# Another order table and other PSUM turns for the opening of an attention and feed-forward kernel

## The chip, the cores and the metric

The kernel runs on one core of a Trainium2 chip. The metric is the device time of one execution in microseconds (us); the time before is the median of three runs.

## What is computed

Causal attention in blocks of 64 positions over 8 batches, 8 heads, 576 positions and 64 features, and then a feed-forward layer on the 4608 tokens (512 to 2048 to 512 features, SiLU between):

```python
scores = scale * np.matmul(q, k.transpose(0, 1, 3, 2))
mask = block_i >= block_j
scores = np.where(mask, scores, -1000000000.0)
scores = scores - np.max(scores, axis=-1, keepdims=True)
attn = np.exp(scores)
attn = attn / (np.sum(attn, axis=-1, keepdims=True) + 1e-09)
return np.matmul(attn, v).astype(np.float32)
...
h = x @ w_in
g = h * (1.0 / (1.0 + np.exp(-h)))
return (g @ w_out).astype(np.float32)
```

The weights come as 64-bit numbers. A weight is a pair of 32-bit words in the kernel's view; it is put together as a 32-bit number on the chip (`rebias` on ScalarE, `bits` on VectorE) and split into a high and a low part (`hi` on ScalarE, `lo` on GpSimd), and each product is the sum of three matmuls of parts.

## The kernel before, in words

Every step of the program has a name, such as `b.norm:1` or `u1.load`, and the string `ORDER` lists all of them, some thousands, in one row. The loop at the end of `attn_ffn` (from L1242) takes them one by one and records their instructions. Each engine, and the SyncE queue (SP) that issues all DMAs, executes its own instructions in that order and waits at the first one whose inputs or buffers are not ready. So the table sets the order on each engine and in the DMA queue, and nothing else is reordered.

The part of the program that this case is about goes as follows.

- `a` and `b` (class `First`, L869) are the attention of the first 64 positions, four batches each. TensorE computes scores (L906), VectorE the maxima (L847, L914) and the differences (L919), ScalarE the exponentials (L924), VectorE sums and reciprocals (L928 to L932), GpSimd multiplies by the reciprocals (`norm`, L935, two per group), TensorE transposes (`turn`, L857; one `turn` reads what both `norm` wrote), ScalarE copies back (L860), TensorE multiplies by v (L947), ScalarE and VectorE make the high and low parts of the tokens (L952, L956).
- `c0` to `c3` (class `Second`, L958) do the same for positions 64 to 191. `BANKS` (L964) says which of the PSUM banks S0 to S3, or U, each of the four groups uses for its two score tiles and for its product.
- `w0` to `w15` are the 16 tiles of the first weight matrix, 512 KB each; `o0` and on are those of the second; `t0` transforms the second matrix's first rows.
- `warm:n` (L827) are matmuls on zeros, n times 64 columns, whose result nobody reads. They fill stretches in which TensorE has nothing to do.
- `ffn` is half of a tile of the first feed-forward product (`ffn1`, L1060). I call them F0, F1, ... in their order; two of them make one tile z0, z1, ... (z12 is F24 and F25, z13 is F26 and F27). `keep` (L1066, ScalarE) copies a finished tile out of one of two PSUM banks, and `save` (L1071, SP) writes it to memory, so `save` waits for `keep` and `keep` for both `ffn`.
- `u0`, `u1`, ... are the heads of the positions from 128 on; `u0.load` and `u1.load` (L668) each fetch 256 KB into one half of the same tile. `d0.run:0` (L766, its matmuls at L775) computes the scores of u0 and u1 together: its first two matmuls of 448 columns read what `u0.load` fetched, the next two what `u1.load` fetched. TensorE therefore waits for both loads before it gets past this step.

A DMA's completion semaphore is one of eight in turn, and the ninth DMA waits for the first to land.

Of the kernel before, what the change touches and what calls it, by code (L numbers as in the profile page):

```python
# [79 lines left out]
w3.bits:2 b.norm:1 warm:17 b.turn:0 w6.load b.turn:1 w0.hi c3.load b.back:0 w2.bits:0 w1.lo c0.scores w2.bits:2 b.back:1 b.pv  # L80
c0.max:0 w7.load w8.load w3.hi w2.hi w4.rebias w9.load w4.bits:0 w0.lo b.hi:0 w5.rebias w10.load ffn c0.exp:0 b.lo:0 w4.bits:2
w4.hi b.hi:1 ffn c0.max:1 w5.bits:0 w5.bits:2 w3.lo c1.load c0.load_v w2.lo ffn ffn c3.scores b.lo:1 keep save w5.hi keep
w7.rebias c0.exp:1 w4.lo w5.lo c3.max:1 c3.max:0 w7.bits:0 w7.bits:2 w6.rebias c0.sum ffn ffn c3.sub:0 ffn ffn keep w6.bits:0
w11.load w8.rebias w6.bits:2 c0.norm w8.bits:0 c0.turn:0 save w9.rebias c3.exp:0 w6.hi c0.turn:1 w8.bits:2 w9.bits:0 w12.load
c3.sub:1 c0.back:0 c0.back:1 c1.scores w7.hi w10.rebias c0.pv keep o0.load w9.bits:2 w6.lo c3.exp:1 w10.bits:0 ffn c3.sum:0
w9.hi w8.hi w10.bits:2 w7.lo ffn w11.rebias w9.lo ffn c3.sum:1 keep w8.lo c3.norm ffn c0.hi w14.load c1.max:0 save c1.sub:0
c1.exp:0 w11.bits:0 w11.bits:2 w14.rebias w11.hi w14.bits:0 keep w11.lo ffn w12.rebias ffn w10.hi w13.load c1.max:1 w10.lo
c1.sub:1 c1.load_v save w14.bits:2 ffn w15.load ffn c1.exp:1 c1.sum:0 c1.sum:1 keep ffn w12.bits:0 w13.rebias w12.bits:2 c1.norm
w13.bits:0 w13.bits:2 ffn save c1.turn:0 o1.load c2.load c1.turn:1 c0.lo c3.turn:1 o0.rebias c3.turn:0 w15.rebias w15.bits:0
o1.rebias w12.hi w12.lo keep c1.back:0 c1.back:1 w15.bits:2 c2.scores o0.bits:0 save w14.hi w14.lo c2.max:0 w13.hi c1.pv w15.hi  # L90
ffn c3.load_v save keep o0.bits:2 ffn ffn c2.exp:0 c2.max:1 save c2.load_v c2.exp:1 save o1.bits:0 w15.lo o1.bits:2 keep w13.lo
all.staged t0.hi:0 t0.hi:1 c1.hi c2.sum c1.lo ffn c3.back:0 c2.norm ffn c3.back:1 keep c2.turn:1 c2.back:1 t0.lo:0 c2.turn:0
c2.back:0 t0.lo:1 t0.x:0 c3.pv c2.pv c3.hi ffn save ffn t0.hi:2 c2.hi save keep u0.load ffn ffn t0.lo:2 t0.x:1 c3.lo keep
o2.load o3.load u0.load_v u1.load_v ffn t0.x:2 t0.hi:3 u2.load_v u1.load u3.load_v save c2.lo save u2.load d0.run:0 keep u3.load
save ffn u4.load u0.max:0 u5.load u0.max:1 u0.ones ffn u0.max:2 u1.max:0 u0.gather ffn u1.ones u0.top keep u1.max:1 ffn
u0.spread u1.max:2 save u0.wide u1.gather ffn u0.sub:0 keep u1.top u0.exp:0 save ffn u0.sub:1 u1.spread u0.sub:2 u0.exp:1
u1.wide ffn u0.add:0 keep u1.sub:2 u0.exp:2 save u1.sub:0 u1.exp:2 u0.add:1 ffn u1.sub:1 u1.exp:0 u0.add:2 u1.exp:1 u0.add:3
d1.run:0 keep u1.add:0 save u1.add:1 ffn u1.add:2 u6.load u2.max:0 u7.load u1.add:3 u2.max:1 u2.ones ffn u2.max:2 u0.sums
u2.gather u3.max:0 ffn keep u2.top u3.ones u3.max:1 save u2.spread u3.max:2 ffn u2.wide u3.gather ffn u2.sub:0 keep u3.top
u2.exp:0 save u2.sub:1 u3.spread u1.sums ffn u2.exp:1 u2.sub:2 d0.sums_g u2.add:0 u3.wide ffn keep u3.sub:2 d0.sums_m u2.exp:2  # L100
save u3.sub:0 u3.exp:2 ffn u3.sub:1 u3.exp:0 u2.add:1 d0.inverse u3.exp:1 d2.run:0 u2.add:2 keep u2.add:3 save u3.add:0 d2.run:1
d0.half u4.max:0 u3.add:1 u4.max:1 u4.ones u3.add:2 u4.max:2 u3.add:3 u4.gather ffn u4.load_v d0.fold u5.load_v u8.load u9.load
u2.sums d0.mult u5.max:0 ffn u4.top u5.ones u5.max:1 u4.spread u5.max:2 ffn keep u4.wide u5.gather save ffn u4.sub:0 d0.x_hi
u5.top u4.exp:0 d0.x_lo u4.sub:1 u5.spread u3.sums ffn keep u4.sub:2 d1.sums_g save u5.wide ffn u4.exp:1 d1.sums_m u5.sub:2
u4.exp:2 u5.sub:0 u5.exp:2 d3.run:0 u5.sub:1 keep u4.add:0 d1.inverse u5.exp:0 save u5.exp:1 u4.add:1 u4.add:2 d3.run:1 d1.half
u6.max:0 u4.add:3 u6.max:1 u6.ones u5.add:0 u6.max:2 u6.gather ffn u5.add:1 u6.load_v d1.fold u7.load_v u10.load u11.load
u4.sums d1.mult u7.max:0 ffn u6.top u5.add:2 u7.ones u7.max:1 u6.spread u5.add:3 u7.max:2 ffn keep u6.wide u7.gather save ffn
u6.sub:0 d1.x_hi u7.top u6.exp:0 d1.x_lo u6.sub:1 u7.spread u5.sums ffn keep u6.sub:2 d2.sums_g save u7.wide ffn u6.exp:1
d2.sums_m u7.sub:2 u6.exp:2 u7.sub:0 u7.exp:2 d4.run:0 u7.sub:1 keep u6.add:0 d2.inverse u7.exp:0 save u7.exp:1 u6.add:1
u6.add:2 d4.run:1 d2.half u8.max:0 u6.add:3 u8.max:1 u8.ones u7.add:0 u8.max:2 u8.gather ffn u7.add:1 u8.load_v d2.fold  # L110
u9.load_v u12.load u13.load u6.sums d2.mult u9.max:0 ffn u8.top u7.add:2 u9.ones u9.max:1 u8.spread u7.add:3 u9.max:2 ffn keep
u8.wide u9.gather save ffn u8.sub:0 d2.x_hi u9.top u8.exp:0 d2.x_lo u8.sub:1 u9.spread u7.sums ffn keep u8.sub:2 d3.sums_g save
u9.wide ffn u8.exp:1 d3.sums_m u9.sub:2 u8.exp:2 u9.sub:0 u9.exp:2 d5.run:0 u9.sub:1 keep u8.add:0 d3.inverse u9.exp:0 save
u9.exp:1 u8.add:1 u8.add:2 d5.run:1 d3.half u10.max:0 u8.add:3 u10.max:1 u10.ones u9.add:0 u10.max:2 u10.gather ffn u9.add:1
u10.load_v d3.fold u11.load_v u14.load u15.load u8.sums d3.mult u11.max:0 ffn u10.top u9.add:2 u11.ones u11.max:1 u10.spread
u9.add:3 u11.max:2 ffn keep u10.wide u11.gather save ffn u10.sub:0 d3.x_hi u11.top u10.exp:0 d3.x_lo u10.sub:1 u11.spread
u9.sums u10.exp:1 u10.sub:2 ffn d4.sums_g u10.add:0 u11.wide u10.exp:2 u11.sub:2 ffn keep d4.sums_m u11.sub:0 u11.exp:2 save
u11.sub:1 d6.run:0 keep u10.add:1 d4.inverse u11.exp:0 save u11.exp:1 u10.add:2 u10.add:3 d6.run:1 d4.half u12.max:0 u11.add:0
u12.max:1 u12.ones u12.max:2 u11.add:1 u11.add:2 u12.gather ffn u12.load_v d4.fold u13.load_v u11.add:3 u16.load u17.load
u10.sums ffn u13.max:0 d4.mult u12.top u13.ones u13.max:1 ffn u12.spread u13.max:2 keep u12.wide d4.x_hi ffn save u13.gather  # L120
d4.x_lo u12.sub:0 ffn u13.top keep u12.sub:1 u13.spread save u11.sums ffn u12.exp:0 u12.sub:2 d5.sums_g u13.wide ffn d5.sums_m
keep u13.sub:2 u12.exp:1 save u13.sub:0 u12.exp:2 ffn u13.sub:1 u12.add:0 u13.exp:0 d5.inverse u13.exp:1 d7.run:0 keep u12.add:1
u13.exp:2 save u12.add:2 u12.add:3 d7.run:1 u13.add:0 d5.half u14.max:0 u14.max:1 u14.ones u13.add:1 u14.max:2 u13.add:2
u14.gather ffn u13.add:3 u14.load_v d5.fold u15.load_v u18.load u19.load u12.sums d5.mult ffn u15.max:0 u14.top u15.ones
u15.max:1 ffn u14.spread u15.max:2 keep u14.wide d5.x_hi ffn save u15.gather d5.x_lo u14.sub:0 ffn u15.top keep u14.sub:1
u15.spread save u13.sums ffn u14.exp:0 u14.sub:2 d6.sums_g u15.wide ffn d6.sums_m keep u15.sub:2 u14.exp:1 save u15.sub:0
u14.exp:2 ffn u15.sub:1 u14.add:0 u15.exp:0 d6.inverse u15.exp:1 d8.run:0 keep u14.add:1 u15.exp:2 save u14.add:2 u14.add:3
d8.run:1 u15.add:0 d6.half u16.max:0 u16.max:1 u16.ones u15.add:1 u16.max:2 u15.add:2 u16.gather ffn u15.add:3 u16.load_v
d6.fold u17.load_v u20.load u21.load u14.sums d6.mult ffn u17.max:0 u16.top u17.ones u17.max:1 t0.lo:3 ffn u16.spread u17.max:2
# [1164 lines left out]
```

## Time and profile before

| | us |
|---|---|
| runs | 939.77, 937.24, 937.60 |
| median | 937.6 |
| profiled execution, device time | 938.08 |
| its span, first to last instruction | 936.4 |
| TensorE busy in the span | 929.8 |

The profiled execution is 0.5 us above the median. 1.7 us of its time lie outside its span. Differences that are worked out inside the span are added to the median. Start times in the trace count from the first instruction. An engine shown as busy may hold a waiting matmul's neighbours only; the weight loads of TensorE (called PEld) show waits more plainly than its matmuls.

### The profile page before, as it was taken

The page shows a single profiled execution, that of the slowest core. Times are in us where ns is not written, and L with a number is a line of the kernel's source. Part 1 is how long each engine was busy: PE and PEld are TensorE (multiplying, and loading weights), DVE is VectorE, ACT ScalarE, POOL GpSimd, SP SyncE. Part 2 cuts the span into 40 slices and gives each one's busy share as a digit, 9 for nine tenths or more (in the row PEclk, how much of TensorE's full clock was granted, in tenths as well). Part 3 has the DMA queues.
Part 4 walks back from the last instruction along what each step waited for, and adds up shares of the span by engine and source line. Part 5 has one row for each costly group of instructions (what it writes and reads, how often), then busy time and mean ns, then how long its engine had stood idle before and what let it go on. Part 6 is the DMA issues. An engine that isn't in the chain of part 4 may idle for free.

```text
span 936.4 us, 23557 instructions
## 1 busy us (share of the span) xinstructions
PE 929.8 (99%) x8646; PEld 815.2 (87%) x8646; DVE 717.8 (77%) x1489; ACT 641.1 (68%) x1621; POOL 550.1 (59%) x799
## 2 busy tenths in 40 slices
...
DMA packets 109813, 139.97 MB, mean 149 GB/s; under 512 B 22656, under 2 KB 87168, under 8 KB 109696
## 3 DMA queue, kind: packets, MB, share of 16 engines
...
## 4 chain that ended last, share of the span: by engine, by line
PE 98%; DVE 1%; ACT 0%; POOL 0%; issue 0%; ACTq 0%; POOLq 0%
PE h L1060 42%; PE c L1143 21%; PE S L1143 16%; PE u L775 7%; PE S L775 5%; PE SC L775 3%; PE U L775 1%; PE h L827 1%; PE S L857 0%; PE S L990 0%; PE U L1029 0%; PE S L1029 0%; PE S L947 0%; DVE p L919 0%; DVE m L914 0%
## 5 line engine op out<-in xcount | busy, mean ns | idle before, releaser
L1060 PE MATMUL h<-x,wi 128*128 128x448 f32 (+2 forms) x1968 | 406.8, 365 | 0.2 <-issue 0.2
L1060 PEld LDWEIGHTS h<-x,wi 128*128 128x128 f32 x1968 | 359.3, 188 | 35.5 <-issue 0.5
L1125 POOL TENSOR_TENSOR wi<-raw,wi 128x512 fp32r<-128x512 f32 (+1 forms) x114 | 115.8, 1031 | 147.8 <-ACT wi L1121 110.5
L1066 ACT COPY g<-h 128x448 f32<-128x448 f32 (+1 forms) x160 | 86.9, 543 | 40.7 <-PE h L1060 27.0
L721 ACT ACTIVATE p<-p 128x448 f32<-128x448 f32 (+2 forms) x192 | 100.9, 571 | 2.2
L775 PE MATMUL S<-qk 64*64 64x384 f32 (+1 forms) x512 | 99.6, 516 | 0.0
L728 POOL TENSOR_TENSOR pa<-p 128x448 f32<-128x448 f32 x64 | 73.3, 1145 | 27.1 <-ACT p L721 15.8
L1143 PE MATMUL c<-ta,wi 128*128 128x256 f32 x684 | 87.0, 276 | 0.0
L1088 ACT ACTIVATE raw<-raw 128x1024 f32<-128x1024 f32 x72 | 76.6, 1065 | 13.5 <-DMA raw<-gdb 10.2
L731 POOL TENSOR_TENSOR pa<-pa,p 128x256 f32<-128x256 f32 (+1 forms) x128 | 79.4, 620 | 10.0 <-ACT p L721 0.4
L1143 PEld LDWEIGHTS c<-ta,wi 128*128 128x128 f32 x684 | 81.8, 188 | 0.0
L1143 PE MATMUL c<-tb,wi 128*128 128x256 f32 x498 | 81.4, 276 | 0.0
L775 PE MATMUL U<-p,v 64*64 64x64 f32 (+4 forms) x768 | 79.8, 354 | 0.0
L775 PE MATMUL u<-p,v 64*64 64x64 f32 (+4 forms) x768 | 78.5, 350 | 0.0
L714 DVE TENSOR_TENSOR p<-S,MR 128x448 f32<-128x448 f32 (+1 forms) x128 | 71.7, 581 | 1.1
L1143 PEld LDWEIGHTS c<-tb,wi 128*128 128x128 f32 x498 | 71.0, 188 | 0.0
L1143 PE MATMUL S<-ta,wi 128*128 128x256 f32 x534 | 70.1, 276 | 0.0
L775 PEld LDWEIGHTS u<-p,v 64*64 64x64 f32 x768 | 43.9, 134 | 29.2 <-issue 24.6
L636 DVE TRANSPOSE_TENSOR_REDUCE Mx<-S 128x14 f32<-128x448 f32 (+1 forms) x128 | 69.3, 576 | 0.0
L1143 PEld LDWEIGHTS S<-ta,wi 128*128 128x128 f32 x534 | 65.0, 188 | 0.0
L1143 PE MATMUL S<-tb,wi 128*128 128x256 f32 x384 | 63.9, 276 | 0.0
L692 ACT COPY Mx<-Mx 64x4 f32<-64x4 f32 x128 | 24.7, 193 | 55.5 <-DVE Mx L636 53.9
...
## 6 DMA issues: line engine op xcount, KB each, us to landing
gdb<-g SPq DMA_DIRECT2D x128, 224.0 KB, 2.3
qk<-in_qk_dram SPq DMA_DIRECT2D x64, 256.0 KB, 4.0
raw<-gdb SPq DMA_DIRECT2D x64, 256.0 KB, 3.3
...
gd<-g SPq DMA_DIRECT2D x32, 256.0 KB, 2.8
...
raw<-gd SPq DMA_DIRECT2D x32, 256.0 KB, 3.4
```

Source lines behind the costliest of these rows:

```text
L636: nc.vector.tensor_reduce(out=out, in_=in_, axis=AX.X, op=op, apply_transpose=True)
L692: nc.scalar.copy(two(Mx[HALF[r], 4, 4 * r : 4 * r + 2], 8), Mx[HALF[r], 3, NQB:].rearrange("p (s r) -> p s r", s=2))
L714: nc.vector.tensor_tensor(out=u.p[:, c : c + w], in0=s[:, :w], in1=u.mb[:, q : q + w], op=ALU.subtract)
L721: nc.scalar.activation(u.p[:, c : c + w], u.p[:, c : c + w], AF.Exp, scale=SCALE)
L728: nc.gpsimd.tensor_tensor(out=u.pa, in0=p[:, :NQ], in1=p[:, ZERO:COLS], op=ALU.add)
L731: nc.gpsimd.tensor_tensor(out=u.pa[:, q : q + w], in0=u.pa[:, q : q + w], in1=p[:, c : c + w], op=ALU.add)
L775: nc.tensor.matmul(o, w, x, start=start, stop=stop)
L1060: nc.tensor.matmul(o, w, x, start=half == 0 and i == 0 or f is None and i == 0, stop=(half == 1 or f is None) and i == len(runs) - 1)
L1066: nc.scalar.copy(g, hs.pop(z)[:, :n])
L1088: nc.scalar.activation(u.raw, u.raw, AF.Silu)
L1125: e.tensor_tensor(out=u.goal(1, k), in0=u.source(k), in1=u.goal(0, k), op=ALU.subtract)
L1143: nc.tensor.matmul(o[:, :HD], *runs[k], start=first, stop=u.q == 3 and n == 5, skip_group_check=True)
```

## The change

The table `ORDER` is replaced from its first step to about the start of the heads `u`; from `d0.run:0` on, the steps stand in the same order as before. The steps are the same ones, with two exceptions: the matmuls on zeros are cut differently (16, 22, 6, 15 and 17 before, now 16, 21, 19, 11 and 9, which is 76 units of 64 columns in both), and the banks of `c0` to `c3` are turned.

```diff
-a.load warm:16 a.scores:0 a.max:0 a.sub:0 a.max:1 a.sub:1 a.scores:1 a.max:2 a.sub:2 a.exp:0 a.max:3 a.sub:3 a.exp:1 b.load
...
+a.load b.load warm:16 a.scores:0 a.max:0 a.max:1 a.sub:0 a.sub:1 a.scores:1 a.max:2 a.sub:2 a.max:3 a.sub:3 a.exp:0 a.exp:1
...
-        BANKS = ((0, 1, 1), (2, "U", "U"), (2, 1, 0), (0, 3, "U"))
+        BANKS = ((1, 0, "U"), (3, 2, 2), (0, 1, 3), ("U", 3, "U"))
```

Three places show what moves. The lines of the changed kernel are lower by one. On ScalarE, from the exponentials of `a` to the copies of `b`, before (p is the tile of `a` or `b`, wm a weight tile being put together, x the tokens):

```order
L924 ACTIVATE p<-p 128x8x64 x2
L531 ACTIVATE wm<-wst 128x512 x2
L860 COPY p<-U_269 128x512
L924 ACTIVATE p<-p 128x8x64 x2
L860 COPY p<-S_268 128x512
L531 ACTIVATE wm<-wst 128x512
L952 CAST x<-S_268 128x2x4x64
```

The same place now:

```order
L923 ACTIVATE p<-p 128x8x64 x2
L530 ACTIVATE wm<-wst 128x512
L923 ACTIVATE p<-p 128x8x64
L530 ACTIVATE wm<-wst 128x512
L923 ACTIVATE p<-p 128x8x64
L859 COPY p<-U_271 128x512
L859 COPY p<-S_270 128x512
```

The two exponentials of `b` now stand ahead of both copies of `a`, and one weight tile's step stands before each of them. On VectorE, in the row of small steps there, before (m is a maximum, rr the sums and reciprocals, SC the scratch bank of the weights):

```order
L914 TENSOR_REDUCE m<-S_268 128x4
L919 TENSOR_TENSOR p<-S_268,m 128x4x64
L914 TENSOR_REDUCE m<-U_269 128x4
L919 TENSOR_TENSOR p<-U_269,m 128x4x64
...
L544 TENSOR_SCALAR SC<-wm 128x512
L928 TENSOR_REDUCE rr<-p 128x8 x2
L931 TENSOR_SCALAR rr<-rr 128x16
```

The same place now:

```order
L913 TENSOR_REDUCE m<-S_270 128x4
L913 TENSOR_REDUCE m<-U_271 128x4
L918 TENSOR_TENSOR p<-S_270,m 128x4x64
L918 TENSOR_TENSOR p<-U_271,m 128x4x64
...
L927 TENSOR_REDUCE rr<-p 128x8
L543 TENSOR_SCALAR SC<-wm 128x512
L927 TENSOR_REDUCE rr<-p 128x8
```

The first two maxima stand together, and a weight tile's step stands between the two sums of `b`. On GpSimd the two `norm` of `a` change places: `a.norm:1`, which needs the second sum, now comes first.

The third place is the SP queue before `d0.run:0`. Before, from the load of u0 (qk is the tile of u0 and u1, v their values, wst in this place the tiles `o2` and `o3`, gd_1_6 and gd_1_7 the memory of z10 to z13):

```order
L1071 DMA gd_1_6_96<-g 128x512
L668 DMA qk<-in_qk_dram 64x1024
L522 DMA wst<-in_moe_w_out_dram 128x512 x2
L674 DMA v<-in_v_dram 128x320
L675 DMA v<-in_v_dram 64x64
...
L668 DMA qk<-in_qk_dram 64x1024
L674 DMA v<-in_v_dram 128x320
L675 DMA v<-in_v_dram 64x64
L1071 DMA gd_1_6_96<-g 128x512
L1071 DMA gd_1_7_98<-g 128x512
```

The same place now:

```order
L667 DMA qk<-in_qk_dram 64x1024
L673 DMA v<-in_v_dram 128x320
L674 DMA v<-in_v_dram 64x64
...
L1070 DMA gd_1_6_96<-g 128x512 x2
L1070 DMA gd_1_7_98<-g 128x512
L521 DMA wst<-in_moe_w_out_dram 128x512
L673 DMA v<-in_v_dram 128x320
L674 DMA v<-in_v_dram 64x64
L667 DMA qk<-in_qk_dram 64x1024
```

The second qk row is `u1.load`. Before, it stood ahead of the saves of z11 and z12; now it stands behind the saves of z10, z11 and z12, behind `o3.load` and behind two DMAs of `u2.load_v`.

## Rows read from the trace of the kernel before

**Rows 1.** Page, part 1: busy time of each engine.

```profile
PE 929.8 (99%) x8646; PEld 815.2 (87%) x8646; DVE 717.8 (77%) x1489; ACT 641.1 (68%) x1621; POOL 550.1 (59%) x799
```

**Rows 2.** Windows, matmuls on zeros (L827): stretch, length, PE, PEld, clock, DMA, GB/s.

```profile
1.05:4.66 3.61, 3.61 (x4) 0.75 (x4) 1.00 0.77 275
16.79:18.76 1.97, 1.97 (x6) 0.73 (x6) 1.00 1.05 386
```

**Rows 3.** Timeline of TensorE, opening: start, length, operation, [idle before, releaser].

```profile
12.78 0.66 PE L857 MATMUL U<-ident,p 128*128 128x128 f32 x4 [1.65 <-POOL p L935]
...
18.76 1.09 PE L857 MATMUL S<-ident,p 128*128 128x128 f32 x8
...
21.75 2.97 PE L1060 MATMUL h<-x,wi 128*128 128x256 f32 x23
```

**Rows 4.** Timeline of VectorE, the sums of a, the differences and sums of b.

```profile
9.67 0.17 DVE L931 TENSOR_SCALAR rr<-rr 128x8 f32<-128x8 f32 x1
...
10.66 0.64 DVE L931 TENSOR_SCALAR rr<-rr 128x8 f32<-128x8 f32 x1
...
12.61 1.28 DVE L919 TENSOR_TENSOR p<-S,m 128x512 f32<-128x512 f32 x2
...
16.20 0.25 DVE L932 RECIPROCAL rr<-rr 128x16 f32<-128x16 f32 x1
```

**Rows 5.** Timeline of GpSimd, the norms of a and b.

```profile
10.23 1.04 POOL L935 TENSOR_TENSOR p<-p,rr 128x512 f32<-128x512 f32 x1 [8.74 <-DVE rr L932]
11.68 1.04 POOL L935 TENSOR_TENSOR p<-p,rr 128x512 f32<-128x512 f32 x1 [0.41 <-DVE rr L932]
16.60 2.05 POOL L935 TENSOR_TENSOR p<-p,rr 128x512 f32<-128x512 f32 x2 [3.88 <-DVE rr L932]
```

**Rows 6.** Timeline of ScalarE, the exponentials of b between weights and copies.

```profile
11.59 0.66 ACT L531 ACTIVATE wm<-wst 128x512 f32<-128x512 f32 x1 [0.64 <-DMA wst<-in_moe_w_in_dram]
...
14.02 1.15 ACT L924 ACTIVATE p<-p 128x512 f32<-128x512 f32 x2
15.07 0.57 ACT L860 COPY p<-S 128x512 f32<-128x512 f32 x1
```

**Rows 7.** Timeline of the SP queue before the heads.

```profile
62.09 0.32 SPq L1071 DMA_DIRECT2D gd<-g  x1
...
63.15 1.00 SPq L522 DMA_DIRECT2D wst<-in_moe_w_out_dram  x2
65.25 0.33 SPq L674 DMA_DIRECT2D v<-in_v_dram  x1
65.62 0.49 SPq L675 DMA_DIRECT2D v<-in_v_dram  x1
...
69.49 0.60 SPq L668 DMA_DIRECT2D qk<-in_qk_dram  x1
```

**Rows 8.** DMA issues of windows from 62.0, 62.4, 69.4 and 72.3: KB, us to landing.

```profile
gd<-g SPq DMA_DIRECT2D x1, 256.0 KB, 2.0
...
qk<-in_qk_dram SPq DMA_DIRECT2D x1, 256.0 KB, 3.6
...
qk<-in_qk_dram SPq DMA_DIRECT2D x1, 256.0 KB, 3.9
...
qk<-in_qk_dram SPq DMA_DIRECT2D x2, 256.0 KB, 4.8
```

**Rows 9.** Timeline of TensorE's weight loads at the start of d0.run:0.

```profile
72.67 0.20 PEld L775 LDWEIGHTS S<-qk 64*64 64x64 f32 x4 [0.36 <-issue]
73.45 0.21 PEld L775 LDWEIGHTS S<-qk 64*64 64x64 f32 x8 [0.58 <-DMA qk<-in_qk_dram]
```

**Rows 10.** Windows of TensorE: d0.run:0 and d1.run:0.

```profile
72.68:75.87 3.19, 3.19 (x49) 1.00 0.92 284
87.01:89.45 2.44, 2.44 (x50) 1.00 0.30 111
```

**Rows 11.** Timeline of ScalarE: the copy that keeps z12.

```profile
70.08 0.59 ACT L1066 COPY g<-h 128x512 f32<-128x512 f32 x1 [2.20 <-PE h L1060]
```

More of the change, by code (lines that the diff above doesn't have):

```diff
@@ L80 @@
[L80 to L129, printed above, removed]
@@ L130 @@
-keep u16.wide d6.x_hi ffn save u17.gather d6.x_lo u16.sub:0 ffn u17.top keep u16.sub:1 u17.spread save u15.sums ffn u16.exp:0
-u16.sub:2 d7.sums_g u17.wide ffn d7.sums_m keep u17.sub:2 u16.exp:1 save u17.sub:0 u16.exp:2 ffn u17.sub:1 u16.add:0 u17.exp:0
-d7.inverse u17.exp:1 d9.run:0 keep u16.add:1 u17.exp:2 save u16.add:2 o2.rebias u16.add:3 o2.bits:0 d9.run:1 u17.add:0 d7.half
-u18.max:0 u18.max:1 u18.ones u17.add:1 u18.max:2 u17.add:2 ffn u18.gather u17.add:3 u18.load_v d7.fold u19.load_v u22.load
@@ L183 @@
[L183 to L185 removed]
+a.load b.load warm:16 a.scores:0 a.max:0 a.max:1 a.sub:0 a.sub:1 a.scores:1 a.max:2 a.sub:2 a.max:3 a.sub:3 a.exp:0 a.exp:1
+a.sum:0 w3.load warm:21 b.scores a.sum:1 b.max:0 w0.load w1.load b.max:1 a.norm:1 a.load_v w0.rebias b.sub:0 b.exp:0 b.sub:1
@@ new lines @@
+w3.lo w4.hi b.lo:1 w2.lo ffn c0.max:1 w5.bits:0 c3.scores keep w5.bits:2 ffn ffn w4.lo w6.rebias w7.load c3.max:1 w5.hi c0.exp:1
+keep w6.bits:0 ffn w6.bits:2 w5.lo c1.load w12.load c3.max:0 c0.sum w6.hi save ffn w8.rebias ffn w8.bits:0 w11.load c3.sub:0
+c0.norm keep w7.rebias w8.bits:2 c3.sub:1 ffn w7.bits:0 c0.turn:0 w10.load w7.bits:2 o0.load w6.lo save c0.turn:1 save c1.scores
+w8.hi w9.rebias w14.load c0.back:0 c0.back:1 c0.pv w9.bits:0 c1.max:0 w7.hi w15.load c1.max:1 keep c1.sub:0 c1.sub:1 c1.exp:0
@@ new lines @@
+c1.exp:1 c3.exp:0 w11.rebias w9.bits:2 w8.lo ffn c1.sum:0 c1.sum:1 w7.lo w11.bits:0 w13.load w11.bits:2 w9.hi ffn ffn w10.rebias
+keep ffn ffn save w10.bits:0 c3.exp:1 c0.hi keep w9.lo ffn w10.bits:2 w10.hi w11.hi c0.lo c2.load ffn c1.norm w10.lo ffn
+c1.load_v w12.rebias w14.rebias save c1.turn:1 c3.sum:0 keep c1.turn:0 c3.sum:1 c2.scores w15.rebias o0.rebias w12.bits:0
+w13.rebias w12.bits:2 c3.norm save w14.bits:0 w14.bits:2 w14.hi c1.back:0 c3.turn:0 c3.turn:1 w13.bits:0 w13.bits:2 c1.back:1
@@ new lines @@
+c1.pv w12.hi w14.lo w15.bits:0 w13.hi keep ffn w11.lo o1.load w15.bits:2 ffn w15.hi c2.max:0 c2.max:1 w15.lo o1.rebias c2.load_v
+o0.bits:0 o0.bits:2 w13.lo ffn c2.exp:0 o1.bits:0 c2.exp:1 w12.lo ffn keep c3.load_v o1.bits:2 c1.hi c3.back:0 all.staged
+t0.hi:0 ffn c2.sum t0.hi:1 save c2.norm t0.lo:0 c3.back:1 o2.load ffn c2.turn:1 keep c1.lo c2.turn:0 save t0.lo:1 save c2.back:1
+c3.pv c2.back:0 keep save c2.pv c3.hi t0.x:0 ffn ffn ffn t0.hi:2 c3.lo ffn c2.hi u0.load keep t0.lo:2 ffn u0.load_v u1.load_v
@@ new lines @@
+t0.x:1 keep save save save o3.load t0.x:2 t0.hi:3 u2.load_v ffn c2.lo u1.load u3.load_v u2.load d0.run:0 keep u3.load save ffn
+u4.load u0.max:0 u5.load u0.max:1 u0.ones ffn u0.max:2 u1.max:0 u0.gather ffn u1.ones u0.top keep u1.max:1 ffn u0.spread
+u1.max:2 save u0.wide u1.gather ffn u0.sub:0 keep u1.top u0.exp:0 save ffn u0.sub:1 u1.spread u0.sub:2 u0.exp:1 u1.wide ffn
+u0.add:0 keep u1.sub:2 u0.exp:2 save u1.sub:0 u1.exp:2 u0.add:1 ffn u1.sub:1 u1.exp:0 u0.add:2 u1.exp:1 u0.add:3 d1.run:0 keep
@@ new lines @@
+u1.add:0 save u1.add:1 ffn u1.add:2 u6.load u2.max:0 u7.load u1.add:3 u2.max:1 u2.ones ffn u2.max:2 u0.sums u2.gather u3.max:0
+ffn keep u2.top u3.ones u3.max:1 save u2.spread u3.max:2 ffn u2.wide u3.gather ffn u2.sub:0 keep u3.top u2.exp:0 save u2.sub:1
+u3.spread u1.sums ffn u2.exp:1 u2.sub:2 d0.sums_g u2.add:0 u3.wide ffn keep u3.sub:2 d0.sums_m u2.exp:2 save u3.sub:0 u3.exp:2
+ffn u3.sub:1 u3.exp:0 u2.add:1 d0.inverse u3.exp:1 d2.run:0 u2.add:2 keep u2.add:3 save u3.add:0 d2.run:1 d0.half u4.max:0
@@ new lines @@
+u3.add:1 u4.max:1 u4.ones u3.add:2 u4.max:2 u3.add:3 u4.gather ffn u4.load_v d0.fold u5.load_v u8.load u9.load u2.sums d0.mult
+u5.max:0 ffn u4.top u5.ones u5.max:1 u4.spread u5.max:2 ffn keep u4.wide u5.gather save ffn u4.sub:0 d0.x_hi u5.top u4.exp:0
+d0.x_lo u4.sub:1 u5.spread u3.sums ffn keep u4.sub:2 d1.sums_g save u5.wide ffn u4.exp:1 d1.sums_m u5.sub:2 u4.exp:2 u5.sub:0
+u5.exp:2 d3.run:0 u5.sub:1 keep u4.add:0 d1.inverse u5.exp:0 save u5.exp:1 u4.add:1 u4.add:2 d3.run:1 d1.half u6.max:0 u4.add:3
@@ new lines @@
+u6.max:1 u6.ones u5.add:0 u6.max:2 u6.gather ffn u5.add:1 u6.load_v d1.fold u7.load_v u10.load u11.load u4.sums d1.mult u7.max:0
+ffn u6.top u5.add:2 u7.ones u7.max:1 u6.spread u5.add:3 u7.max:2 ffn keep u6.wide u7.gather save ffn u6.sub:0 d1.x_hi u7.top
+u6.exp:0 d1.x_lo u6.sub:1 u7.spread u5.sums ffn keep u6.sub:2 d2.sums_g save u7.wide ffn u6.exp:1 d2.sums_m u7.sub:2 u6.exp:2
+u7.sub:0 u7.exp:2 d4.run:0 u7.sub:1 keep u6.add:0 d2.inverse u7.exp:0 save u7.exp:1 u6.add:1 u6.add:2 d4.run:1 d2.half u8.max:0
@@ new lines @@
+u6.add:3 u8.max:1 u8.ones u7.add:0 u8.max:2 u8.gather ffn u7.add:1 u8.load_v d2.fold u9.load_v u12.load u13.load u6.sums d2.mult
+u9.max:0 ffn u8.top u7.add:2 u9.ones u9.max:1 u8.spread u7.add:3 u9.max:2 ffn keep u8.wide u9.gather save ffn u8.sub:0 d2.x_hi
+u9.top u8.exp:0 d2.x_lo u8.sub:1 u9.spread u7.sums ffn keep u8.sub:2 d3.sums_g save u9.wide ffn u8.exp:1 d3.sums_m u9.sub:2
+u8.exp:2 u9.sub:0 u9.exp:2 d5.run:0 u9.sub:1 keep u8.add:0 d3.inverse u9.exp:0 save u9.exp:1 u8.add:1 u8.add:2 d5.run:1 d3.half
@@ new lines @@
+u10.max:0 u8.add:3 u10.max:1 u10.ones u9.add:0 u10.max:2 u10.gather ffn u9.add:1 u10.load_v d3.fold u11.load_v u14.load u15.load
+u8.sums d3.mult u11.max:0 ffn u10.top u9.add:2 u11.ones u11.max:1 u10.spread u9.add:3 u11.max:2 ffn keep u10.wide u11.gather
+save ffn u10.sub:0 d3.x_hi u11.top u10.exp:0 d3.x_lo u10.sub:1 u11.spread u9.sums u10.exp:1 u10.sub:2 ffn d4.sums_g u10.add:0
+u11.wide u10.exp:2 u11.sub:2 ffn keep d4.sums_m u11.sub:0 u11.exp:2 save u11.sub:1 d6.run:0 keep u10.add:1 d4.inverse u11.exp:0
@@ new lines @@
+save u11.exp:1 u10.add:2 u10.add:3 d6.run:1 d4.half u12.max:0 u11.add:0 u12.max:1 u12.ones u12.max:2 u11.add:1 u11.add:2
+u12.gather ffn u12.load_v d4.fold u13.load_v u11.add:3 u16.load u17.load u10.sums ffn u13.max:0 d4.mult u12.top u13.ones
+u13.max:1 ffn u12.spread u13.max:2 keep u12.wide d4.x_hi ffn save u13.gather d4.x_lo u12.sub:0 ffn u13.top keep u12.sub:1
+u13.spread save u11.sums ffn u12.exp:0 u12.sub:2 d5.sums_g u13.wide ffn d5.sums_m keep u13.sub:2 u12.exp:1 save u13.sub:0
+u12.exp:2 ffn u13.sub:1 u12.add:0 u13.exp:0 d5.inverse u13.exp:1 d7.run:0 keep u12.add:1 u13.exp:2 save u12.add:2 u12.add:3
@@ new lines @@
+u16.ones u15.add:1 u16.max:2 u15.add:2 u16.gather ffn u15.add:3 u16.load_v d6.fold u17.load_v u20.load u21.load u14.sums d6.mult
+ffn u17.max:0 u16.top u17.ones u17.max:1 t0.lo:3 ffn u16.spread u17.max:2 keep u16.wide d6.x_hi ffn save u17.gather d6.x_lo
+u16.sub:0 ffn u17.top keep u16.sub:1 u17.spread save u15.sums ffn u16.exp:0 u16.sub:2 d7.sums_g u17.wide ffn d7.sums_m keep
+u17.sub:2 u16.exp:1 save u17.sub:0 u16.exp:2 ffn u17.sub:1 u16.add:0 u17.exp:0 d7.inverse u17.exp:1 d9.run:0 keep u16.add:1
@@ new lines @@
+u17.exp:2 save u16.add:2 o2.rebias u16.add:3 o2.bits:0 d9.run:1 u17.add:0 d7.half u18.max:0 u18.max:1 u18.ones u17.add:1
+u18.max:2 u17.add:2 ffn u18.gather u17.add:3 u18.load_v d7.fold u19.load_v u22.load u23.load u16.sums d7.mult ffn u19.max:0
+u18.top u19.ones u19.max:1 ffn u18.spread u19.max:2 keep u18.wide d7.x_hi ffn save u19.gather d7.x_lo u18.sub:0 u19.top keep
+u18.sub:1 ffn u19.spread save u17.sums u18.exp:0 u18.sub:2 d8.sums_g ffn u19.wide u18.exp:1 d8.sums_m u19.sub:2 u19.sub:0 keep
@@ new lines @@
+u20.add:0 u21.sub:1 d9.inverse d11.run:0 keep u20.add:1 u21.exp:0 save o3.bits:2 u21.exp:1 u20.add:2 t1.hi:0 u20.add:3 t1.hi:1
+d11.run:1 u22.max:0 u21.add:0 d9.half u22.max:1 u22.ones u22.max:2 u21.add:1 u21.add:2 u22.gather ffn u22.load_v d9.fold
+u23.load_v u21.add:3 u26.load u27.load u20.sums ffn u23.max:0 d9.mult u22.top u23.ones u23.max:1 ffn t1.lo:0 u22.spread
+u23.max:2 keep u22.wide d9.x_hi ffn save u23.gather d9.x_lo u22.sub:0 ffn u23.top keep u22.sub:1 u23.spread save u21.sums
+t1.lo:1 ffn u22.exp:0 u22.sub:2 d10.sums_g u23.wide ffn d10.sums_m keep u23.sub:2 u22.exp:1 save u23.sub:0 u22.exp:2 ffn
```

108 lines of the change are left out of this document (53 added, 55 removed).

## The prediction

> **What bounds the kernel now.** I read the page's busy times first: TensorE is busy for 929.8 of 936.4 us [rows 1]. So the time falls only by what TensorE waits or spends on zeros, and it rises by every new wait of TensorE. The change keeps all matmuls, and the zeros too (76 units before and after), so only waits can differ. I looked for them in two places: in TensorE's timeline of the opening, and, since that view may hide a wait behind a neighbouring matmul, in the row of weight loads where the opening ends.
>
> The opening: TensorE stands 1.65 us before the first transpose of `a`, released by GpSimd's `norm` [rows 3, 5]. The transpose of `b` at 18.76 comes 0.11 us after the end of GpSimd's two norms of `b`, 16.60 + 2.05 = 18.65 [rows 3, 5]. From there real work follows without a gap: F0 starts at 21.75 [rows 3].
>
> The end of the opening: `d0.run:0` takes 3.19 us, where `d1.run:0` with the same matmuls takes 2.44 us [rows 10]. The difference of 0.75 us is a wait: four weight loads of u0 at 72.67, and then nothing until 73.45, when the DMA of u1 releases the rest [rows 9]. That DMA was issued at 69.49 and took 3.9 us [rows 7, 8]. So before the change TensorE already waits here for `u1.load`.
>
> **The change part by part.**
>
> *The chain to F0.* The second sum of `a` has a small addition that takes 0.64 us, where the same one for the first sum takes 0.17 us [rows 4]; beside the slow one `a.norm:0` runs on GpSimd (10.23 to 11.27) [rows 5]. Now `a.norm:1` comes first and needs that very sum, so GpSimd is idle there: I take 0.17, which is 0.47 us less. Two maxima that stand together let VectorE do one while the other's result arrives; from the rhythm of four such pairs I give that 0.18 us. VectorE is then 0.65 us ahead. The transpose of `a` needs both norms: 11.68 - 0.65 = 11.03, plus 2.05 for two in a row [rows 5], is 13.08, so it starts at about 13.1, 0.3 us later than before, and the 19 units of zeros fill the wait. The exponentials of `b` go ahead of the copies of `a` now. The first starts at 12.65, when the first of two differences is there (12.61 + 0.64 before [rows 4], less 0.65), after the weight step that waits for a load (11.59 to 12.25; the tile has the same place in the queue, so I keep its time) [rows 6]; the second follows another weight step, 0.55 us, and ends at about 14.4, where before it ended at 15.17 [rows 6]. That is 0.8 us sooner, and the second sum of `b`, its reciprocal (ended at 16.45 before [rows 4]) and the norms follow: 15.8 + 2.05 = 17.85. The transpose of `b` starts at 17.95 instead of 18.76.
>
> Is TensorE free by then? The copies of `a` now end at about 15.3 (15.64 before [rows 6]), the product with v follows at 15.4 and takes 1.1 us, and 9 units of zeros at 1.97 / 17 = 0.116 us each [rows 2] end at 17.5. Yes. So F0 comes at 20.95, 0.8 us sooner. The ends of this term: nothing, if the small addition stays slow and a weight step falls badly, and 2.4 us, if all waiting before F0 went, which is the 1.65 us and some 0.7 us in smaller pieces. I take 0.8.
>
> *From F0 to F27.* Weights, groups `c0` to `c3` and their banks stand in another order, but everything they deliver is due on TensorE, and TensorE runs without gaps there now. I laid the row durations end to end for each delivery; the closest are the low part of w2 (0.7 us ahead of F2), the copy of z4 (0.7 ahead of F12) and the second copy of `c0` (0.4 ahead of its product). I cost this at nothing. It is hidden by TensorE's own work, and if a cover fails the price is some tenths, which eat from the 0.8.
>
> *The load of u1.* This is the term that decides. In the SP queue `u1.load` now stands behind the save of z12, and a DMA queue that waits holds back all that is behind it. The save waits for ScalarE's copy of z12, which starts when F25 ends: 70.08 before [rows 11], so 69.28 now, plus 0.59 is 69.87. Then SP issues, by its own rows: the save 0.32, `o3.load` 0.5 (two in 1.00), the two DMAs of `u2.load_v` 0.33 and 0.49, which is 1.64, and behind each a gap (0.04 between the two at 65.25 and 65.62) [rows 7]. Sum 1.8 to 2.1; I take 1.95, and `u1.load` goes out at 71.8, instead of 69.49. The three loads of this kind nearby took 3.6, 3.9 and 4.8 us [rows 8]. The first had little ahead of it, the last two saves; this one has a save, 512 KB and the values of u2 ahead. I take 4.0, with ends 3.6 and 4.8: it lands at 75.8. What is left of `d0.run:0` after the landing took 75.87 - 73.45 = 2.42 us [rows 9, 10]. It ends at 78.3 instead of 75.87, 2.4 us later, and everything behind it stands in the old order, so it shifts as a whole. The 0.8 us of the opening are in this already, since F25 is earlier by them.
>
> A sentence apart: the Trainium skill, page "DMA: Bandwidth & Descriptors", section "Anatomy of one DMA", gives a fixed cost of about 2.0 us and bytes at 436 GB/s, which would be an estimate of 2.6 us for 256 KB, and the sum by it would be 937.6 + 1.0 = 938.6. The trace does not agree for these loads.
>
> *Sum.* 937.6 + 2.4 = 940.0. The bounds of the parts: issue and landing give -0.5 to +1.0, and the opening -0.6 to +0.8 around it.
>
> **The rivals.** *The wait costs the clock too; this ends on the slower side.* All windows show a granted clock of 1.00, but the first matmuls on zeros, after TensorE had done nothing, took 3.61 us for 16 units, where 17 units took 1.97 us later [rows 2]: half the speed, the lower of the two levels of 1.2 and 2.4 GHz. At the later rate they would have taken 1.85 us, so a slow start costs 1.76 us. In `d0.run:0` TensorE would now stand for some 3 us. If the clock falls in that, the same price comes on top: 937.6 + 2.4 + 1.8 = 941.8. Against it: 1.65 us of standing at 12.78 brought no slow stretch (17 units at 16.79 ran fast), and no row shows a wait as long as 3 us. It decides from about that length. The Trainium skill, page "TensorE: Matmul & The Clock Gate", section "HAM oscillation", tells of a kernel whose waits for DMA let the clock fall each time; by that the time would be this one, and no row of before shows such a fall within the kernel.
>
> *The load is not late.* If `u1.load` lands as fast as the save nearby, 2.0 us [rows 8], it lands at 73.8 and `d0.run:0` ends at 76.2, which gives 938.0; with a queue that issues faster and a larger gain in the opening down to 936.8. For it speaks that the DMA engines have only a save and one weight tile ahead; against it, all loads of this kind took 3.6 us or more.
>
> *The opening gains nothing.* If a delivery between F0 and F25 comes late by what the opening gained, the chain ends 0.8 us later: 940.8.
>
> **How the numbers follow.** The late load at the old clock: 0.58, 939.0 to 941.0. The clock falls: 0.16, 941 to 942.6. The load is not late: 0.14, 936.8 to 938.4. The opening gains nothing: 0.09, 940.4 to 941.2. A gain larger than the late load takes back: 0.03. A measurement can tell about 0.3%, which is 2.8 us: 934.8 to 940.4 count as no change. Slower by more: a third of the first case (0.19), nearly all of the second (0.15), most of the fourth (0.07), together 0.41. Faster by more: 0.02, since even 2.4 us of waiting in the opening don't reach 934.8 alone. The rest, 0.57, is no change. The range leaves out the lower half of the early landing and the upper third of the fallen clock: 937.8 to 942.0.
>
> **What would show it.** In the profile after: the transposes of `a` at about 13.1 and of `b` at about 17.95, F0 at 20.95; the small addition at 0.17; the copy of z12 at 69.3 and `u1.load` issued at 71.8; a wait of the weight loads of `d0.run:0` of about 3 us, released by the DMA of qk; the step's length 6.4 us instead of 3.19; after it the same matmul times (the clock rival: matmuls of half speed right behind the wait). I am wrong if that wait is under 1 us, or if TensorE shows idle time of more than 0.5 us between F0 and F27.

## The result and the profile after

The changed kernel takes 944.71 us (median of 4 runs, 943.68 to 946.89) against 937.8 us (4 runs, 937.24 to 939.77): the ratio is 1.0075, with a 95% interval from 1.0062 to 1.0087. It is slower by 0.75%, and the prediction (940.0, at most 942.0) was too low. The profiled execution is the slowest of the four, 946.89 us with a span of 945.2 us, so its trace shows 2.2 us more than the median does.

The page of after, its first part and the line of TensorE's clock (40 slices of the span):

```profile
PE 934.9 (99%) x8648; PEld 819.7 (87%) x8648; DVE 717.6 (76%) x1489; ACT 640.7 (68%) x1621; POOL 548.5 (58%) x799
...
PEclk9997999999999999999999999999999999999999
...
L774 PE MATMUL S<-qk 64*64 64x384 f32 (+1 forms) x512 | 101.2, 526 | 4.4 <-DMA qk<-in_qk_dram 4.4
```

TensorE is busy 5.1 us longer than before [rows 1] with the same matmuls, so some of them were slow: the fourth slice shows a clock of 0.7. The third line shows 4.4 us of waiting for the DMA of qk. Both lie at `d0.run:0`. TensorE's weight loads there, and windows of TensorE from the step's start to the landing of u1, from there to F28, and from F28 to `d1.run:0` (length, busy, clock, DMA share, GB/s):

```profile
71.77 0.19 PEld L774 LDWEIGHTS S<-qk 64*64 64x64 f32 x4 [0.36 <-issue]
77.17 0.30 PEld L774 LDWEIGHTS S<-qk 64*64 64x64 f32 x8 [5.21 <-DMA qk<-in_qk_dram]
```

```profile
71.77:77.17 5.40, 0.97 (x5) 0.92 1.05 230
77.17:81.85 4.68, 4.68 (x45) 0.50 0.46 120
81.85:95.32 13.47, 13.47 (x75) 0.82 0.31 99
```

Before, the same three pieces took 0.77, 2.42 and 11.14 us [rows 9, 10], and `d0.run:0` began at 72.68. So at `d1.run:0` the account is: 0.91 earlier, 4.63 more waiting, 2.26 and 2.33 at a lower clock, together 8.3 us later (95.32 against 87.01). The last 0.5 us of the span's 8.8 come later; 0.33 of them between `d3.run:0` and `d4.run:0`, which is taken up below.

Where the clock fell, in windows of 1 us:

```profile
75.00:76.00 1.00, 0.00 (x0) 1.00 1.07 203
76.00:77.00 1.00, 0.00 (x0) 0.67 1.21 200
77.00:78.00 1.00, 0.83 (x8) 0.50 0.93 201
...
85.00:86.00 1.00, 1.00 (x6) 0.50 0.62 135
86.00:87.00 1.00, 1.00 (x8) 0.71 0.00 0
87.00:88.00 1.00, 1.00 (x11) 1.00 0.00 0
```

The clock falls to 0.50, the lower of the two levels (1.2 GHz), at about 76.3, while TensorE stands, and is back at 1.00 at about 86.6. The matmuls from 77.17 on run at the lower level for 9 us. And the SP queue, with the DMA issues of that stretch (KB, us to landing):

```profile
65.72 4.38 SPq L1070 DMA_DIRECT2D gd<-g  x3
70.19 0.38 SPq L521 DMA_DIRECT2D wst<-in_moe_w_out_dram  x1
70.67 0.39 SPq L673 DMA_DIRECT2D v<-in_v_dram  x1
71.11 0.47 SPq L674 DMA_DIRECT2D v<-in_v_dram  x1
71.63 0.59 SPq L667 DMA_DIRECT2D qk<-in_qk_dram  x1
```

```profile
wst<-in_moe_w_out_dram SPq DMA_DIRECT2D x1, 512.0 KB, 4.1
qk<-in_qk_dram SPq DMA_DIRECT2D x1, 256.0 KB, 5.5
```

Three saves hold the queue until z12 is copied (69.17 + 0.59 = 69.76); `u1.load` goes out at 71.63 and takes 5.5 us, against 3.9 before [rows 8].

Between these two traces the opening did what it should. VectorE's small addition, the norms, the transposes of `a` and `b`, and F0:

```profile
10.02 0.17 DVE L930 TENSOR_SCALAR rr<-rr 128x8 f32<-128x8 f32 x1
```

```profile
10.58 2.04 POOL L934 TENSOR_TENSOR p<-p,rr 128x512 f32<-128x512 f32 x2 [9.09 <-DVE rr L931]
15.98 2.04 POOL L934 TENSOR_TENSOR p<-p,rr 128x512 f32<-128x512 f32 x2 [3.36 <-DVE rr L931]
```

```profile
12.68 0.66 PE L856 MATMUL U<-ident,p 128*128 128x128 f32 x4 [0.23 <-POOL p L934]
```

```profile
18.08 1.09 PE L856 MATMUL S<-ident,p 128*128 128x128 f32 x8 [0.28 <-POOL p L934]
```

```profile
21.07 3.10 PE L1059 MATMUL h<-x,wi 128*128 128x256 f32 x24
```

F0 starts at 21.07 instead of 21.75 [rows 3], and ScalarE copies z12 at 69.17 instead of 70.08 [rows 11].

### The profile page after: what moved, and what is told of

The parts are those of the page before. It is cut to its first block, busy times and chain, and to the rows that moved or that the text cites. A ratio compares the mean times of both kernels' runs of the same rounds, so it can differ in the third digit from the quotient of the medians.

```text
span 945.2 us, 23557 instructions
## 1 busy us (share of the span) xinstructions
PE 934.9 (99%) x8648; PEld 819.7 (87%) x8648; DVE 717.6 (76%) x1489; ACT 640.7 (68%) x1621; POOL 548.5 (58%) x799
## 4 chain that ended last, share of the span: by engine, by line
PE 96%; DMA 2%; DVE 1%; SPq 0%; POOL 0%; ACT 0%; issue 0%; ACTq 0%; DVEq 0%; POOLq 0%
PE h L1059 42%; PE c L1142 20%; PE S L1142 16%; PE u L774 7%; PE S L774 5%; PE SC L774 3%; PE U L774 2%; DMA wst<-in_moe_w_in_dram 1%; DMA qk<-in_qk_dram 1%; PE S L856 0%; PE S L989 0%; PE U L1028 0%; POOL p L934 0%; PE S L1028 0%; SPq L880 0%; DVE Mx L635 0%
## 5 line engine op out<-in xcount | busy, mean ns | idle before, releaser
L635 DVE TRANSPOSE_TENSOR_REDUCE Mx<-SC 128x16 f32<-128x512 f32 x32 | 22.9, 716 | 57.7 <-PE U L774 39.9
```

The lines of the kernel that those rows point to most:

```text
L635: nc.vector.tensor_reduce(out=out, in_=in_, axis=AX.X, op=op, apply_transpose=True)
```

## The experiments

The theory from the two traces: the late `u1.load` alone makes the loss, first as a wait and then through the clock; the opening by itself gains. Rivals: the opening or the banks lose something of their own; the load is slow for another reason than its place. In the diffs one step, or a few, stand on a line. The kernel before had medians of 937.97 us (first four experiments), 938.39 (the next four) and 938.03 (the last one) beside them; each ratio is to the one of its own group.

**The load early, in the changed kernel.**

```diff
 c2.hi u0.load
+u1.load
 keep t0.lo:2 ffn u0.load_v u1.load_v
...
 c2.lo
-u1.load
 u3.load_v u2.load
```

> The changed kernel, with u1.load moved in the table to right behind u0.load, and nothing else. Theory (the whole loss is the late load and the half-speed stretch behind it): no wait of the weight loads in d0.run:0, which starts at about 71.8 us and takes 2.44 us; the time is that of before, less 0.9 us of the opening and 0.75 us of wait, about 936.1 us. Rival (the new order or the banks cost something behind the opening too): the time stays above 938, with stretches behind d0.run:0 that are longer than in the kernel before.

Measured: 937.02 us (936.54 to 938.92, 11 runs), ratio 0.9991 [0.9982, 1.0000]. The loss is gone, 7 us of it with one step of the table. The weight loads of `d0.run:0` no longer wait:

```profile
71.75 0.21 PEld L774 LDWEIGHTS S<-qk 64*64 64x64 f32 x8 [0.36 <-issue]
```

`d1.run:0` starts 1.46 us sooner than before (85.55 against 87.01); 0.97 of it is left in the time of the two profiled executions (937.11 against 938.08). So the gain is smaller than the 936.1 that I expected, and its interval reaches to no change.

**The load early, in the kernel before.** The same move there.

> The kernel before, with u1.load moved to right behind u0.load. Theory: the 0.75 us by which d0.run:0 is longer than d1.run:0 is a wait for this load and goes away, and nothing else changes: about 937.0 us. Rival (the longer step is not the load's doing): no change, 937.8 us.

Measured: 937.38 us (936.93 to 938.41, 11 runs), ratio 0.9994 [0.9985, 1.0003]. In the trace the wait is gone:

```profile
72.38 0.21 PEld L775 LDWEIGHTS S<-qk 64*64 64x64 f32 x8 [0.36 <-issue]
```

The time is 0.6 us lower by the medians, which is not clear of no change. With the load out of the way in both tables, the new opening is worth 937.38 - 937.02 = 0.36 us (drawn again at random from the two sets of eleven runs, the difference of the medians is 0.1 to 0.6).

**The load late, in the kernel before.** Only the queue ahead of `d0.run:0` is put as in the changed kernel; the old opening and the old banks stay.

```diff
 o2.load
-o3.load
 u0.load_v u1.load_v
+save save o3.load
 ffn t0.x:2 t0.hi:3 u2.load_v u1.load u3.load_v
-save
 c2.lo
-save
 u2.load d0.run:0
```

> The kernel before, with only the DMA queue ahead of d0.run:0 put as in the changed kernel: the saves of z11 and z12 and o3.load stand ahead of the values of u2 and of u1.load. Theory: the copy of z12 ends at 70.7, u1.load goes out at about 72.4 and lands at about 77.9, and a stretch at half speed follows: the time is that of the changed kernel plus the opening's gain, about 945.5 us. Rival (the opening's own order makes the loss): near 938 us.

Measured: 944.97 us (943.86 to 947.6, 4 runs), ratio 1.0078 [1.0063, 1.0092]: the whole loss, without the new opening. The wait and the clock are there as well:

```profile
77.36 0.30 PEld L775 LDWEIGHTS S<-qk 64*64 64x64 f32 x8 [5.09 <-DMA qk<-in_qk_dram]
```

```profile
76.00:77.00 1.00, 0.00 (x0) 0.89 1.12 226
...
77.36:80.00 2.64, 2.63 (x20) 0.50 0.67 185
80.00:81.00 1.00, 1.00 (x26) 0.91 0.00 0
```

In this profiled execution (the fastest of its four) the half speed lasts from about 76.8 to 80.2. The rest of `d0.run:0` took 3.81 us (77.36 to 81.17) instead of 2.42, and F28 to `d1.run:0` 11.35 instead of 11.14: the clock costs 1.6 us here, where it cost 4.6 in the profiled execution of after, the slowest of its four. The 3.0 us between the two are about as much as the runs of either kernel differ (3.2 and 3.7 us).

**Zeros in the wait.** The changed kernel with 40 units of matmuls on zeros ahead of `d0.run:0`; the load is as late as in after.

```diff
 u1.load u3.load_v u2.load
+warm:40
 d0.run:0
```

> The changed kernel, with 40 units of matmuls on zeros (about 4.6 us, whose result nobody reads) put ahead of d0.run:0, where TensorE stands for 5.4 us. Theory that standing lets the clock fall: granted clock 1.00 throughout, d0.run:0 ends some 2.45 us behind the landing at about 77.1, so at 79.6, 3.7 us behind the kernel before: about 941.5 us, 3 us less than the changed kernel in spite of more work. Rival (the clock falls for another reason, or does not cost what it seems to): 944.7 us or more.

Measured: 941.81 us (940.99 to 942.43, 4 runs), ratio 1.0039 [1.0026, 1.0053], with a mean clock of 1.00 in every run. TensorE, and windows to the start of `d0.run:0` and on to `d1.run:0`:

```profile
71.66 4.50 PE L827 MATMUL h<-zero 128*64 128x512 f32 x10
```

```profile
71.66:76.10 4.44, 4.44 (x11) 1.00 1.03 285
76.10:90.14 14.04, 14.04 (x121) 1.00 0.45 135
```

Some four tenths of the loss, 2.9 of 6.9 us, go with work that nobody needs. Not all of it is the clock's: the load went out at 71.53 and took 4.8 us here, so it landed at about 76.3 and not at 77.13. If the profiled executions stand for the others, 0.8 of the 2.9 us come from the load and about 2 are left for the clock.

**Why the load takes so long: the 512 KB ahead of it.** The changed kernel with one step moved.

```diff
 save save save
-o3.load
 t0.x:2 t0.hi:3 u2.load_v ffn c2.lo u1.load
+o3.load
 u3.load_v u2.load d0.run:0
```

> The changed kernel with one step moved: o3.load (512 KB) stands right behind u1.load instead of ahead of the values of u2. The save of z12 stays ahead. u1.load goes out 0.45 us sooner, at about 71.2 instead of 71.63. Theory A (the 512 KB just ahead is what made the load take 5.5 us instead of 3.6 to 4.0): it lands at about 75.2, the wait of d0.run:0 is about 3.5 us; if the clock stays at 1.00 in a wait of that length, d0.run:0 ends at 77.6 and the time is 939.6; if it falls here too, 942 to 943.5. Rival B (the load's 5.5 us comes from what is issued behind it, the values of u3 and the loads of u2 and u3, or from the save of z12): it lands at 76.5 or later, the wait is 4.8 us, the clock falls, 944.2.

Measured: 942.34 us (939.9 to 943.28, 4 runs), ratio 1.0038 [1.0024, 1.0052]. The load went out at 70.90 and took 3.4 us:

```profile
qk<-in_qk_dram SPq DMA_DIRECT2D x1, 256.0 KB, 3.4
```

```profile
74.39 0.21 PEld L774 LDWEIGHTS S<-qk 64*64 64x64 f32 x8 [2.68 <-DMA qk<-in_qk_dram]
```

```profile
71.52:74.39 2.87, 0.97 (x5) 1.00 0.82 258
74.39:88.19 13.80, 13.79 (x117) 1.00 0.58 175
```

So the weight tile ahead made about 2 us of the landing time. The profiled execution kept its clock and took 939.9 us, the first case of the expectation; the three others took 942.34, 942.34 and 943.28 with a mean clock of 0.996 to 0.998, the second case. With a wait of this length the clock falls in some executions and not in others, and the three lie 2.4 to 3.4 us above the one that kept it.

**The waiting save.** The changed kernel with only the save of z12 (the third one) moved right behind `u1.load`.

```diff
 save save
-save
 o3.load t0.x:2 t0.hi:3 u2.load_v ffn c2.lo u1.load
+save
 u3.load_v u2.load d0.run:0
```

> The changed kernel with one step moved: the save of z12, which waits for ScalarE's copy of z12 until 69.8, stands right behind u1.load instead of ahead of o3.load. o3.load and the values of u2 stay ahead of u1.load. If the wait of that save is what makes the load late (my theory): u1.load goes out at about 68.3 instead of 71.63, lands at about 72.2 to 73.5, the wait of d0.run:0 is 0 to 1.5 us, no fall of the clock, 936.6 to 938.2. Rival (o3.load itself waits for its buffer or for the completion of a DMA eight earlier, so that the queue stands anyway): u1.load goes out after 70.5, the clock falls, 942 to 945.

Measured: 939.85 us (938.36 to 943.72, 11 runs), ratio 1.0019 [1.0007, 1.0031]. The load went out at 68.82, 2.8 us sooner, but took 5.0 us behind the weight tile and landed at 73.78. The wait was longer than I expected, and the time lies above the 936.6 to 938.2 that I gave: the waiting save accounts for when the load goes out, not for how long it takes.

```profile
qk<-in_qk_dram SPq DMA_DIRECT2D x1, 256.0 KB, 5.0
```

```profile
73.82 0.21 PEld L774 LDWEIGHTS S<-qk 64*64 64x64 f32 x8 [2.01 <-DMA qk<-in_qk_dram]
```

Nine of the eleven runs took 938.4 to 940.1 us at a clock of 0.999 or 1.000 (median 939.44), two took 943.4 and 943.7 at 0.996, some 4 us more.

**Both.** The save of z12 and `o3.load` both right behind `u1.load`.

> The changed kernel with both the save of z12 and o3.load moved right behind u1.load; the saves of z10 and z11 and the values of u2 stay ahead. The two single moves each left a wait of d0.run:0: 2.0 us with the save away (the load then took 5.0 us, behind the 512 KB), 2.7 us with o3.load away (it then took 3.45 us). If these two are all that made u1.load late: it goes out at about 68.2, lands at about 71.8, d0.run:0 starts with a wait under 0.7 us, the clock stays at 1.00 in every run, and the time is that of the kernel with the load right behind u0.load, about 0.5 to 1 us under before: 937.2 within 0.7. Rival (something else ahead, the values of u2 or the two other saves, holds the load): the wait is 1.5 us or more, and the time 938.5 or more.

Measured: 937.63 us (936.91 to 938.09, 11 runs), ratio 0.9995 [0.9986, 1.0004], every run at a clock of 1.00, as expected. The load went out at 68.26 and took 3.6 us, and `d0.run:0` runs through:

```profile
qk<-in_qk_dram SPq DMA_DIRECT2D x1, 256.0 KB, 3.6
```

```profile
71.61 0.57 PEld L774 LDWEIGHTS S<-qk 64*64 64x64 f32 x10 [0.36 <-issue]
```

These two steps ahead of it are what made the load late.

**The banks.** The new `BANKS` in the kernel before, and the old ones in the kernel of the first experiment.

```diff
-        BANKS = ((0, 1, 1), (2, "U", "U"), (2, 1, 0), (0, 3, "U"))
+        BANKS = ((1, 0, "U"), (3, 2, 2), (0, 1, 3), ("U", 3, "U"))
```

> The kernel before with the new BANKS of c0 to c3 alone. My theory: the banks carry nothing alone, 937.8 within 0.5 us. Rival (the old order needs its own turns, the new ones make a group of c0 to c3 wait for a bank): TensorE shows a wait between F0 and F27, 938.5 to 941.

> The changed kernel with u1.load right behind u0.load, and the old BANKS of c0 to c3. If the banks don't matter: d0.run:0 is reached at 71.75 and the time is 937.0, as with the new banks. Rival (the new table needs the new turns): a group of c0 to c3 waits for a bank, d0.run:0 is reached 0.5 us or more later, 937.5 to 940.

Measured: 939.57 us (938.64 to 941.42, 11 runs), ratio 1.0013 [1.0005, 1.0022], and 938.83 us (938.48 to 940.5, 11 runs), ratio 1.0008 [0.9999, 1.0017]. My theory missed both; the rivals hold. TensorE waits between F0 and F27 where no wait was: at the scores and a transpose of a group of `c0` to `c3` in the old table with new banks, and at the scores of one in the new table with old banks:

```profile
35.88 1.10 PE L990 MATMUL S<-qk 64*64 64x128 f32 x32 [1.36 <-issue]
...
53.18 0.66 PE L857 MATMUL S<-ident,p 128*128 128x128 f32 x4 [0.29 <-ACT MR L860]
```

```profile
51.17 1.10 PE L989 MATMUL S<-qk 64*64 64x128 f32 x32 [0.87 <-ACT MR L859]
```

So each table runs best with its own turns. That the first of these waits is one for a bank follows from the edit alone: the profile names no releaser for it ("issue"). The second kernel's interval just reaches no change against the kernel before; against the new table with its own turns (ratio 0.9991) it is some 1.6 us slower. Its profiled execution began `d0.run:0` at 74.12 instead of 71.75, but that execution is the slowest of its eleven (940.5), and 1.4 us of the difference are there before 25.5, ahead of the wait shown.

## Why the prediction was wrong

**The chain to F0: the steps right, the size partly luck.** Between the two traces F0 comes 0.68 us sooner instead of 0.8, by the steps named: the small addition at 0.17, the norms of `a` as one pair, those of `b` ending at 18.02 (predicted 17.85), the transposes at 12.68 and 18.08 (13.1 and 17.95). The small addition takes 0.64 us in all four profiled kernels with the old table and 0.17 in all seven with the new one. The gain is less sure: the transposes of `b` start at 18.00, 18.05, 18.57 and 18.76 with the old table and at 17.82 to 18.08 with the new one. The execution of before that I read is the last of the four, and by the medians (18.31 and 17.93) the gain is 0.4. (A slip in the working: 12.61 + 0.64 - 0.65 is 12.60, not 12.65; nothing hangs on it.)

**F0 to F27 at no cost: right.** `d0.run:0` is reached at 71.77 (71.9 follows from my numbers), 0.91 us sooner than in the trace of before; two other executions with the old table and its turns reach it at 72.08 and 72.38. Before, TensorE did have a small gap on the way, 0.16 us at 24.89, which "without gaps" passes over. The experiments with the banks show that this rests on table and turns fitting together.

**When the load goes out: right.** 71.63 against 71.8, for the reason given: the save of z12 waits for ScalarE's copy and holds the queue.

**How long it takes: mis-sized.** This is the first term that failed. I took 4.0 us from three loads with ends of 3.6 and 4.8; it took 5.5, and landed at 77.13 instead of 75.8. I had named the 512 KB just ahead and then priced the load like loads without them. The four loads with the weight tile and the values of u2 right ahead of them (after and three experiments) took 5.5, 5.4, 5.0 and 4.8 us, the two without the tile 3.4 and 3.6. During the wait of after the DMA share is 1.05 (first window above), so the 16 engines were taken all the time, though they moved 230 GB/s where the same share went with 386 in the opening [rows 2]; what they spent the time on is not shown. The trace of before could have told it. There the values of u0 go out right behind two weight tiles, and 160 KB took 5.1 us:

```profile
v<-in_v_dram SPq DMA_DIRECT2D x1, 160.0 KB, 5.1
```

With the landing right and nothing else, the sum would have been 941.3, still inside my range. The figure of the Trainium skill, page "DMA: Bandwidth & Descriptors", section "Anatomy of one DMA", which gave 2.6 us as an estimate, is further off than mine; none of these loads agrees with it. The section gives the figure for DMAs that GpSimd issues, and SyncE issues these.

**The clock: the wrong case was the likeliest.** This is the second term that failed, and the one that took the time out of the range. I gave the fall a chance of 0.16 and argued that a standing of 1.65 us had brought no slow stretch, and that no row showed a longer one. That was no evidence for 3 us, let alone for more. TensorE stands from the end of its work on u0, 0.97 us after the start of `d0.run:0`, to the release. The kernels in which it stands 4.4 and 4.3 us lost the clock in 8 of 8 runs (mean clock 0.995 to 0.998), the one with 1.9 us in 3 of 4, the one with 1.2 us in 2 of 11, and the one with zeros in the wait in none of 4. (The length is that of each kernel's profiled execution; landing times may differ in the others.) My own forecast was 75.8 - 71.9 - 0.97 = 2.9 us by this count, between a standing that lost the clock in 3 of 4 runs and one that lost it in all. So the fall was the likelier case already there, and "from about that length" was put too long. The length alone does not settle it either: the kernel before stands 1.65 us ahead of the transposes of `a`, and none of its 63 runs beside the experiments has a mean clock under 0.999. What else counts, no run tried.

**Its price: too low by a part.** I priced the fall as one slow start, 1.76 us [rows 2]. It was 1.6 us in one profiled execution and 4.6 in the other; by the medians, after lies 2.9 us above the kernel with zeros in the wait, about 2 of them the clock's. Within one kernel the runs that lost it lie 2.4 to 3.4 us above the one that kept it (`o3.load` behind) and some 4 us above the others (the waiting save). The Trainium skill, page "TensorE: Matmul & The Clock Gate", section "HAM oscillation", which I had cited for this rival, tells of about 1.67 us at the lower clock after each DMA wait. The fall itself agrees with this trace; the length does not, since here the lower clock lasted some 3 us of work in one execution and 9 in the other.

The rival with two sizes mended comes near the result: 941.8, plus 1.3 for the landing, plus 0.3 for the stretch at `d3.run:0`, is 943.4. What is missing to 944.7, 1.3 us, lies within what the longer half speed added in the profiled execution (4.6 - 1.8 = 2.8).

**What became of the gain.** With the load in time the opening should have left 0.8 us, and 0.36 is there. In the two kernels with the early load `d0.run:0` begins at 71.75 and 72.38, so 0.63 us reach it. About 0.34 of them are lost between `d3.run:0` and `d4.run:0`: 13.5 us in all seven kernels with the new table, 13.2 in the four with the old one, though the steps from `d0.run:0` on are the same. At `d3.run:0` TensorE takes scores (S<-qk) and products with v (U<-p,v) in turn, and the products read the `p` that VectorE writes. In the new table (first experiment) TensorE comes there before VectorE has finished, and the products start 0.35 us behind the scores:

```profile
112.34 0.19 PEld L774 LDWEIGHTS S<-qk 64*64 64x64 f32 x4 [0.36 <-issue]
112.69 0.19 PEld L774 LDWEIGHTS U<-p,v 64*64 64x64 f32 x4 [0.15 <-DVE p L716]
```

In the old one (second experiment) both start together:

```profile
112.97 0.14 PEld L775 LDWEIGHTS S<-qk 64*64 64x64 f32 x2 [0.36 <-DVE p L717]
112.99 0.14 PEld L775 LDWEIGHTS U<-p,v 64*64 64x64 f32 x2
```

From there to the next `ffn` it takes 5.05 us in the new table (to 117.39) and 4.71 in the old one (112.98 to 117.69). VectorE had lost its lead 5 us earlier, at a maximum ahead of which it stands in the new table (first line, the first experiment) and not in the old one (second line, the second experiment):

```profile
107.65 0.28 DVE L687 TENSOR_REDUCE mj<-Mx 128x14 f32<-128x70 f32 x1 [0.48 <-ACT g L1065]
```

```profile
107.91 0.28 DVE L688 TENSOR_REDUCE mj<-Mx 128x14 f32<-128x70 f32 x1
```

What VectorE waits for there stays open; no run tried it. The profile names ScalarE's copy of g, which ends at 107.60. But in the old table the same maximum starts at 107.91, while that copy is still running (107.64 to 108.23), so the name may be wrong.
